# A planned instruction order that accounts for the SBUF port of GpSimd and VectorE, with first-layer weight sums moved into the attention part

## The chip, the cores and the metric

The kernel runs on one core of a Trainium2 chip. TensorE (PE) multiplies matrices, VectorE (DVE) and ScalarE (ACT) do elementwise work and read the matmul results in PSUM, GpSimd (POOL) does elementwise work on SBUF alone, and SyncE (SP) issues the DMAs. Each engine runs its own instructions in the order of the program and waits on semaphores for the others. The metric is device time in microseconds from the first to the last instruction; of several runs the median counts.

## The reference

An attention with decay is followed by a token mix and a dense layer pair; all weights of the second part (`U`, `V`, `w_ch1`, `w_ch2`) come as 64-bit floats, all else as 32-bit floats.

```python
batch, n_heads, seq, head_dim = (8, 8, 576, 64)          # d_model 512, rank 32
def _attn_ref(q, k, v, f):
    scores = scale * np.matmul(q, k.transpose(0, 1, 3, 2))
    cum = np.cumsum(np.log(np.clip(f, 0.0001, 1.0)), axis=-1)
    scores = np.where(causal, -1000000000.0, scores + cum[:, :, :, None] - cum[:, :, None, :])
    attn = np.exp(scores - np.max(scores, axis=-1, keepdims=True))
    attn = attn / (np.sum(attn, axis=-1, keepdims=True) + 1e-09)
    return np.matmul(attn, v)
def _moe_ref(x, U, V, w_ch1, w_ch2):                      # x: (8, 576, 512)
    u = x + (x.transpose(0, 2, 1) @ U @ V).transpose(0, 2, 1)
    return u + np.maximum(u @ w_ch1, 0.0) @ w_ch2         # 512 -> 2048 -> 512
```

## The kernel before, in words

A matmul operand is held as a high part and a low part (names that end in h and l), and a product is three matmuls: high by high, low by high, high by low.

The first part works through 32 pairs of heads, four to a batch. A pair's scores go to PSUM (tiles `S`), VectorE adds the decay and mask `M` and finds the row limit `nm` (L543, and L578 for the last 64 rows), ScalarE takes the exponent (L549), PE turns the result (L616) into PSUM tiles `T`, and a copy brings it to `PT` (line L267, on ScalarE or VectorE). PE multiplies by the values, and the normalised result lands in `xn`. `split_x` splits it, `ranks` makes the rank sums `TS` (L724 on VectorE). When a batch has its four pairs, `mix` adds the token mix to `xn` (PE L733, VectorE L734) and turns the result (PE L749, and L760 for the last 64 rows) into `uh` (a copy) and `ul` (L742 on VectorE). `dense` then does the first 6 of the 16 hidden chunks for that batch: L795 into PSUM, `hh` by ScalarE, `hl` by VectorE (L799), L816 back, and `ost` (L833). This dense work of the batch before is what PE does between the attention matmuls of the next.

The other ten chunks of both weights are prepared meanwhile by `ahead(r, i)` (r is 1 for the first layer's weight): 64-bit words are loaded into `araw`, decoded and stored to DRAM as `wd`. A decode, `decode_ops`, is a chain: a scaling (L375 on VectorE), `signs` (L385, L386) and `rest` (L390, L391), both on VectorE alone, an addition (L401), a copy (L409 or L410) and a subtraction (L405); the last three and the scaling may go to one of two engines. After the attention the second part loads `wd`, and `weight_sums` makes four sums per pair of first-layer chunks, which a block scheme with seven products uses in the third part, up to the end.

None of this order is written out. `op` notes a piece of work with its keys, its priority and its engines with a duration for each. `run` keeps a clock for each engine and again and again takes, over all engines, the piece that could begin first, by these durations and a fixed lag per engine; `fn()` then writes its instructions. So the order on each engine is fixed when the program is built, and on the chip nothing but semaphores for data keeps two engines in step. While dense work has not begun, `run` fills planned waits of PE with dummy matmuls (`keep_awake`, L856).

Of the kernel before, what the change touches and what calls it, by code (L numbers as in the profile page):

```python
# [48 lines left out]
def tile_decay_attention_moe(ctx, tc, qk, v, f, U, V, w1, w2, out):  # L49
# [312 lines left out]
    def decode_ops(pr, n, get, kr, ka, kw, rows=slice(0, 128)):  # L362
# [45 lines left out]
        op([
            ("ACT", 0.06 + 0.5 * k, lambda: nc.scalar.copy(views()[5], views()[3])),  # L409
            ("DVE", 0.06 + 0.27 * k, lambda: nc.vector.tensor_copy(views()[5], views()[3])),  # L410
        ], pr, ka, kw)
        op(both(low), pr, ka, kw)
# [549 lines left out]
    staged = [0]  # L962

    def weight_sums(i, pr):
        free = xn[(B - 2) % NX]
        homes = ((free[:, 2], X(B - 2, 2)), (free[:, 3], X(B - 2, 3)), (xn[(B - 3) % NX][:, NM], X(B - 3, NM)))
        a0, a1 = (xn[(B - 3) % NX][:, (2 * k + 1) % NM] for k in (2 * i, 2 * i + 1))
        k0, k1 = (X(B - 3, (2 * k + 1) % NM) for k in (2 * i, 2 * i + 1))
        for k, a, ka in ((2 * i, a0, k0), (2 * i + 1, a1, k1)):
            h, l = (w[k].bitcast(F32).rearrange("p c f -> p (c f)") for w in (b1h, b1l))  # L970
            whole = lambda e, a=a, h=h, l=l: e.tensor_tensor(a, h, l, op=ALU.add)
            op([("POOL", 1.23, lambda whole=whole: whole(nc.gpsimd)), ("DVE", 0.6, lambda whole=whole: whole(nc.vector))], pr, [("b1", k, x) for x in range(2)], ka)
        lo, hi = slice(0, 256), slice(256, 512)
        t = [free[:, x // 2, 256 * (x % 2) : 256 * (x % 2) + 256] for x in range(4)]
        ks = [X(B - 2, x // 2, x % 2) for x in range(4)]
        ops = (
            (0, t[0], a1[:, lo], a1[:, hi], ALU.add, k1), (1, t[1], t[0], a0[:, lo], ALU.subtract, k0 + ks[0]),
# [616 lines left out]
```

## Time and profile before

| what | value |
| --- | --- |
| median of 3 runs | 1205.87 us (1203.4 to 1208.3) |
| the profiled execution | 1211.09 us, of which its instructions span 1209.3 us |
| busy over the span | PE 96%, VectorE 63%, ScalarE 58%, GpSimd 32% |
| mean granted TensorE clock | 0.986 |

The first part fills the span up to about 690 us, the seven-product part most of what follows 790 us. A busy PE is not PE at its peak, since matmuls overlap and their ends are modelled; the waits of PE and the stretches in which its clock was halved tell more than the busy share.

### The profile page before, as it was taken

To read this page: it belongs to the slowest core of one execution; us is meant where nothing else is said; L and a number is where in the kernel's file an instruction comes from. 1 tells how busy PE (TensorE), PEld (TensorE's weight loads), DVE (VectorE), ACT (ScalarE), POOL (GpSimd) and SP (SyncE) were. 2 spreads that over 40 slices of the span, in tenths; PEclk is the share of its full clock that TensorE was granted. 3 is DMA by queue.
4 is the path that set the end of the run, shared out by engine and by line. 5 is a ranking of instruction groups with operands and counts; after the bars stand their busy time and mean duration, and the time that the engine had idled before them with its cause. 6 is when DMAs were issued, how large, how long until landed. Compare 5 with 4: busy or idle time off the path is not lost.

```text
span 1209.3 us, 23833 instructions
## 1 busy us (share of the span) xinstructions
PE 1163.5 (96%) x8370; PEld 1005.7 (83%) x8370; DVE 767.4 (63%) x1856; ACT 699.3 (58%) x1891; POOL 385.1 (32%) x512
## 2 busy tenths in 40 slices
PE   9889999999999999989999899999999999999998
PEld 5557778877868878778887798888999999999997
DVE  7888676575573664764654322248768778687765
ACT  8776666666765666655756321146555655555553
POOL 5676644555643554543633353100000000000000
PEclk9989999999999999989999999999999999999999
DMA  6654546656555355454451576647765564654643
GB/s 206 169 172 160 170 135 180 164 162 189 175 144 199 112 192 180 136 194 134 131 162 34 168 247 217 222 156 246 253 207 181 168 236 153 231 197 153 201 114 105
DMA packets 133448, 210.32 MB, mean 174 GB/s; under 512 B 16656, under 2 KB 58896, under 8 KB 131280
## 3 DMA queue, kind: packets, MB, share of 16 engines
q1 hardware_dynamic: 133056, 208.53, 55.1%
q8 instruction: 66, 1.08, 0.4%
q14 instruction: 54, 0.44, 0.1%
q10 hardware_dynamic: 272, 0.26, 0.1%
HBM read 153.03 MB, written 55.72 MB: 173 GB/s over the span
## 4 chain that ended last, share of the span: by engine, by line
PE 75%; DVE 11%; issue 4%; ACT 4%; DMA 3%; POOL 1%; SPq 1%; POOLq 0%; DVEq 0%; ACTq 0%
PE pf L1234 16%; PE F L795 9%; PE po L1326 8%; PE F L816 7%; PE T L653 6%; PE px L1326 4%; PE S L525 4%; PE T L616 3%; PE F L1052 2%; PE O L1074 2%; PE pf L1326 2%; DVE S L543 2%; ACT P L549 2%; PE po L1341 2%; PE T L635 1%
## 5 line engine op out<-in xcount | busy, mean ns | idle before, releaser
L549 ACT ACTIVATE P<-S,nm 128x512 f32<-128x512 f32 (+3 forms) x256 | 133.0, 530 | 58.0 <-DVE nm L543 57.6
L543 DVE CUSTOM_DVE_ANT_0 S<-S,M 128x512 f32<-128x512 f32 (+3 forms) x256 | 119.7, 516 | 53.3 <-PE S L525 46.3
L1385 POOL TENSOR_TENSOR xn<-xn,xn 128x512 f32<-128x512 f32 x1 | 1.3, 1267 | 411.7 <-DMA out_dram<-xn 411.7
L501 POOL TENSOR_SCALAR_AFFINE_SELECT M<-decay 128x1024 f32<-128x1024 f32 (+1 forms) x124 | 96.0, 788 | 106.6 <-DVE nm L543 88.9
L267 ACT COPY PT<-T 128x512 f32<-128x512 f32 (+4 forms) x282 | 113.6, 449 | 24.6 <-PE T L616 13.7
L795 PE MATMUL F<-uh,w1h 128*128 128x256 f32 (+1 forms) x352 | 113.7, 323 | 7.1 <-DVE hl L799 5.3
L795 PE MATMUL F<-uh,w1l 128*128 128x256 f32 (+1 forms) x352 | 106.0, 301 | 0.0
L795 PE MATMUL F<-ul,w1h 128*128 128x256 f32 (+1 forms) x352 | 106.0, 301 | 0.0
L616 PE MATMUL T<-ident,P 128*128 128x128 f32 x612 | 88.8, 279 | 8.0 <-ACT PT L267 2.4
L1457 ACT COPY ost<-pf 128x512 f32<-128x512 f32 x70 | 41.1, 587 | 87.3 <-PE pf L1234 87.3
L653 PE MATMUL T<-PT,vr 128*64 128x320 f32 (+3 forms) x628 | 91.1, 437 | 0.0
L616 PEld LDWEIGHTS T<-ident,P 128*128 128x128 f32 x612 | 71.3, 142 | 22.6 <-ACT PT L267 5.0
L1457 ACT COPY mc<-pf 128x512 f32<-128x512 f32 x69 | 40.5, 587 | 81.6 <-PE pf L1234 81.6
L484 POOL TENSOR_TENSOR qkl<-raw,qkh 128x576 fp32r<-128x576 f32 (+1 forms) x52 | 79.8, 1538 | 18.8 <-ACT qkh L483 13.1
L799 DVE SCALAR_TENSOR_TENSOR hl<-F,hh 128x256 fp32r<-128x256 f32 (+1 forms) x88 | 39.6, 451 | 69.2 <-ACT hh L804 68.6
L653 PEld LDWEIGHTS T<-PT,vr 128*64 128x64 f32 x628 | 41.2, 139 | 46.3 <-issue 35.8
L795 PEld LDWEIGHTS F<-uh,w1h 128*128 128x128 f32 x352 | 69.6, 198 | 11.5 <-DVE hl L799 6.2
L816 PE MATMUL F<-w2h,hh 128*128 128x512 f32 x180 | 77.1, 428 | 0.1
L704 POOL TENSOR_TENSOR xl<-xn,xh 128x512 fp32r<-128x512 f32 x32 | 42.2, 1320 | 91.4 <-ACT xh L701 48.9
L816 PE MATMUL F<-w2l,hh 128*128 128x512 f32 x180 | 71.1, 395 | 0.0
L816 PE MATMUL F<-w2h,hl 128*128 128x512 f32 x180 | 70.5, 392 | 0.0
L795 PEld LDWEIGHTS F<-uh,w1l 128*128 128x128 f32 x352 | 69.5, 198 | 0.0
(330 smaller groups left out, 3618.0 us busy)
## 6 DMA issues: line engine op xcount, KB each, us to landing
un<-ud SPq DMA_DIRECT2D x16, 1024.0 KB, 6.8
decay<-cumd SPq DMA_DIRECT2D x30, 512.0 KB, 5.9
d<-ud SPq DMA_DIRECT2D x48, 256.0 KB, 4.0
araw<-in_w_dram SPq DMA_DIRECT2D x20, 512.0 KB, 4.3
wd<-araw SPq DMA_DIRECT2D x20, 512.0 KB, 3.3
twd<-xn SPq DMA_DIRECT2D x40, 256.0 KB, 2.8
raw<-in_qk_dram SPq DMA_DIRECT2D x32, 288.0 KB, 4.1
Th<-twd SPq DMA_DIRECT2D x35, 256.0 KB, 3.3
```

The lines of the kernel that those rows point to most:

```text
L267: return [("ACT", 0.133 + 0.00068 * n, lambda: nc.scalar.copy(dst(), src())), ("DVE", 0.064 + 0.00104 * n, lambda: nc.vector.tensor_copy(d ...
L484: op([("POOL", 0.1 + 0.00225 * n, lambda c=c: nc.gpsimd.tensor_tensor(l[:, c], raw[:, c], h.bitcast(F32)[:, c], op=ALU.subtract))], p - 0. ...
L501: nc.gpsimd.affine_select(Ms[i], decay[:, :, 0:w], [[0, 2], [-1, w]], ALU.is_ge, MASKED, base=P * i, channel_multiplier=1)
L543: nc.vector.tensor_tensor_reduce(ps, ps, Ms[i][:, j], scale=-SCALE, scalar=3.0e38, op0=ALU.add, op1=ALU.min, accum_out=nm[:, col : col + 1],)
L549: nc.scalar.activation(PP[i][j], bank[j][:, off : off + w], AF.Exp, bias=nm[:, col : col + 1], scale=-1.0, accum_out=sm[:, col : col + 1])
L616: nc.tensor.transpose(bank[:, P * x : P * x + P], PP[i][j][:, P * c : P * c + P], ident)
L653: nc.tensor.matmul(ps, vr[:, c, j], PT[:, j, c, lo:hi], start=c == 0, stop=lo == 0)
L795: nc.tensor.matmul(bank[:, :nt], wt[:, fc, c], ut[:, c, sl], start=m == 0, stop=m == 3 * NDC - 1)
L816: nc.tensor.matmul(bank[:, :], ht[:, fc, P * y : P * y + P], wt[:, fc], start=fc == 0 and m == 0, stop=fc == NA - 1 and m == 2,)
L1234: nc.tensor.matmul(ps, a[x][:, c], b[y][:, c], start=start and m == 0, stop=m == 5, skip_group_check=True)
L1326: nc.tensor.matmul(ps[:, HT * x : HT * x + HT], f[a][:, P * x : P * x + P], w[b], start=k.i == 0 and m == 0 and x == 0 and not (k.n == NG ...
L1457: nc.scalar.copy(mc, FA)
```

## The change

It has four parts. (1) In the planner, GpSimd does not begin before the stretch in which VectorE holds the shared SBUF port has passed (`hold["DVE"]`), and a VectorE piece that carries a fourth number, the time for which it holds the port, does not begin before GpSimd is done (`hold["POOL"]`). (2) Durations on VectorE are raised, every result counts as ready 0.1 us later for its readers (`CUSH`), a decode step's another 0.4 us (`EASE`; 1.2 us behind the scaling, which reads a DMA's landing), and a change of PE's mode costs more priority (`TURN`). (3) The rule `LAZY` goes, by which VectorE took a piece that another engine may do only where that engine was 0.6 us behind. (4) `weight_sums` goes; `sums_ahead` makes the same sums from the decoded chunks while they are still in SBUF, behind every second first-layer chunk, and the order of the chunks is changed so that two first-layer ones stand together.

```diff
-TURN = 0.08
+TURN = 0.15
...
 SHY = 0.6
-LAZY = {"ACT": 0.6, "POOL": 0.6}
+EASE = 0.4
+CUSH = {"PE": 0.1, "DVE": 0.1, "ACT": 0.1, "POOL": 0.1, "SP": 0.1}
+BEHIND = 1.0
+AT, SPAN = 7, 22
...
+                    for eng, dur, fn, *port in o.alts:
                         if eng != e:
                             continue
-                        if e == "DVE" and len(o.alts) > 1:
-                            other = "ACT" if o.alts[0][0] == "ACT" or o.alts[1][0] == "ACT" else "POOL"
-                            if clock[other] < max(now, o.ready) + LAZY[other]:
-                                continue
                         est = max(now, o.ready)
+                        if e == "POOL":
+                            est = max(est, hold["DVE"])
+                        if port:
+                            est = max(est, hold["POOL"])
...
             clock[e] = end
+            if e == "POOL":
+                hold["POOL"] = end
+            if port:
+                hold["DVE"] = est + port[0]
...
-                    x.ready = max(x.ready, done)
+                    x.ready = max(x.ready, done + x.ease + CUSH[x.alts[0][0]])
...
-        op([("DVE", 0.1 + 0.9 * k, signs)], pr, (), ka + kr)
-        op([("DVE", 0.1 + 0.9 * k, rest)], pr, ka, kr)
+        op([("DVE", 0.14 + k, signs, 0.43 * k)], pr, (), ka + kr, ease=ease)
+        op([("DVE", 0.14 + k, rest, 0.43 * k)], pr, ka, kr, ease=ease)
 
         def both(fn):
-            return [("POOL", 0.1 + 1.13 * k, lambda: fn(nc.gpsimd)), ("DVE", 0.06 + 0.54 * k, lambda: fn(nc.vector))]
+            return [("POOL", 0.14 + 1.13 * k, lambda: fn(nc.gpsimd)), ("DVE", 0.08 + 0.6 * k, lambda: fn(nc.vector), 0.69 * k)]
 
...
-        ka = [("araw",)]
+        ka = [("araw", x) for x in range(3)]
+        own, ko = ((late_a, ("warm",)), (late_b, ("late",)))[r and i % 2]
         load(pr - 0.5, 512e3, lambda: nc.sync.dma_start(araw, (w1_src if r else w2_src)(NA + i)), w=ka)
         h, l = (araw[:, DM * x : DM * x + DM].bitcast(F32R) for x in range(2))
-        decode_ops(pr, 512, lambda: (araw.rearrange("p (n t) -> p n t", t=2), late_a[:, :], h, l), ka, [("warm",)], ka)
+        decode_ops(pr, 512, lambda: (araw.rearrange("p (n t) -> p n t", t=2), own[:, :], h, l), ka, [ko], ka, ease=EASE)
         load(pr, 524e3, lambda: nc.sync.dma_start(wd[r, i].rearrange("x p d -> p x d"), araw.bitcast(F32).rearrange("p (x d) -> p x d", x=2)), r=ka, w=[("wd", r, i)])
+
+    def sums_ahead(m, pr):
+        lo, hi = slice(0, 256), slice(256, 512)
+        fl32 = lambda t, sl: t[:, sl].bitcast(F32)
+        t = [lambda: fl32(araw, lo), lambda: fl32(araw, hi), lambda: fl32(late_b, lo), lambda: fl32(late_a, hi)]
+        b_hi, a_lo = lambda: fl32(late_b, hi), lambda: fl32(late_a, lo)
+        kt = [("araw", 0), ("araw", 1), ("late",), ("warm",)]
+
+        def both(n, fn):
+            return [("POOL", 0.14 + 1.13 * n, lambda: fn(nc.gpsimd)), ("DVE", 0.08 + 0.6 * n, lambda: fn(nc.vector), 0.69 * n)]
+
+        for n, x, y, o, kr in (
+            (0, t[2], b_hi, ALU.add, [("late",)]), (1, t[0], a_lo, ALU.subtract, [("araw", 0), ("warm",)]),
+            (2, a_lo, t[2], ALU.subtract, [("warm",)]), (3, t[3], t[1], ALU.subtract, [("araw", 1)]),
+        ):
+            op(both(0.5, lambda e, n=n, x=x, y=y, o=o: e.tensor_tensor(t[n](), x(), y(), op=o)), pr, kr, [kt[n]], ease=EASE)
+        homes = ((araw[:, 512:1024].bitcast(F32), ("araw", 2)), (spare_home, ("sum",)))
+        for x in range(4):
+            q, kh = homes[x % 2]
+            qr = q.bitcast(F32R)
+            op([("ACT", 0.36, lambda x=x, qr=qr: nc.scalar.copy(qr[:, lo], t[x]()))], pr, [kt[x]], [kh], ease=EASE)
+            low = lambda e, x=x, q=q, qr=qr: e.tensor_tensor(qr[:, hi], t[x](), q[:, lo], op=ALU.subtract)
+            op(both(0.5, low), pr, [kt[x]], [kh], ease=EASE)
+            load(pr, 262e3, lambda x=x, q=q: nc.sync.dma_start(twd[0, m, x], q), r=[kh], w=[("twd", m, x)])
 
...
-            TURNS.setdefault(7 + k * 22 // (2 * NB), []).append((1 - k % 2, k // 2))
+            TURNS.setdefault(AT + k * SPAN // (2 * NB), []).append((1 - k % 4 // 2, k // 4 * 2 + k % 2))
...
-                    ahead(r, i, p + 1.0)
+                    ahead(r, i, p + BEHIND)
+                    if r and i % 2:
+                        sums_ahead(i // 2, p + BEHIND)
...
-    def weight_sums(i, pr):
-        free = xn[(B - 2) % NX]
...
-            if i % 2:
-                weight_sums(i // 2, 41.0 + i)
```

Other durations are changed alike. Counted over the whole program, VectorE has 216 more instructions and ScalarE 167 fewer, GpSimd 59 fewer: 148 copies and 5 casts of L267 move from ScalarE to VectorE, as do 12 casts and 2 scalings of decodes, and 29 additions and subtractions of decodes and `split_x` move from GpSimd to VectorE. PE's instructions are the same but for 18 more dummy matmuls and as many weight loads, and the order on PE is nearly the same. The lines of the changed kernel stand some 10 lower (L742 is L752 there), and tile numbers behind a name differ.

At the end of the attention, VectorE's order before was this (the `mix` of the last batch; `xn_98` is that batch, `b1h` and `b1l` are the second part's weights, which DMAs bring):

```order
L833 TENSOR_TENSOR ost_134<-F_144,xn_97 128x512 [waits DMAHW7_49,PE_49]
L734 TENSOR_TENSOR xn_98<-S_138,xn_98 128x512 [waits PE_49,Pool_49]
L734 TENSOR_TENSOR xn_98<-S_139,xn_98 128x512 [waits PE_49]
L734 TENSOR_TENSOR xn_98<-S_140,xn_98 128x512 [waits PE_49]
L734 TENSOR_TENSOR xn_98<-S_141,xn_98 128x512 [waits PE_49]
L971 TENSOR_TENSOR xn_99<-b1h_7306,b1l_7316 128x512 [waits DMAHW4_49,DMAHW3_49,Pool_49]
L742 TENSOR_TENSOR ul<-F_145,uh 128x4x128 [waits DMAHW0_49,Activation_49]
L742 TENSOR_TENSOR ul<-T_142,uh 128x4x128 [waits Activation_49]
L734 TENSOR_TENSOR xn_98<-F_144,xn_98 64x512 [waits DVE_49,PE_49]
L742 TENSOR_TENSOR ul<-S_138,uh 128x4x128 [waits Activation_49]
```

and in the changed kernel it is this:

```order
L734 TENSOR_TENSOR TS<-T_145,TS 32x256 [waits Activation_49]
L744 TENSOR_TENSOR xn_98<-S_142,xn_98 128x512 [waits PE_49,Pool_49]
L843 TENSOR_TENSOR ost_136<-F_147,xn_97 128x512 [waits DMAHW0_49,PE_49]
L744 TENSOR_TENSOR xn_98<-S_143,xn_98 128x512 [waits PE_49]
L744 TENSOR_TENSOR xn_98<-S_141,xn_98 128x512 [waits PE_49]
L752 TENSOR_TENSOR ul<-S_140,uh 128x4x128 [waits DMAHW6_49,Activation_49]
L744 TENSOR_TENSOR xn_98<-T_144,xn_98 128x512 [waits PE_49]
L744 TENSOR_TENSOR xn_98<-T_145,xn_98 64x512 [waits DVE_49,PE_49]
L272 CAST uh<-F_147 128x4x128 [waits PE_49]
L752 TENSOR_TENSOR ul<-S_142,uh 128x4x128 [waits Activation_49]
L752 TENSOR_TENSOR ul<-F_147,uh 128x4x128 [waits DVE_49]
L752 TENSOR_TENSOR ul<-S_143,uh 128x4x128 [waits Activation_49]
```

The sum of two loaded weights (L971) that stood among the `mix` steps is gone, and one of the `uh` copies is VectorE's now.

In the `mix` of a middle batch (the sixth), VectorE's order before was this (`araw` and `w2a` are a decode's):

```order
L385 TENSOR_SCALAR araw<-araw 128x512 [waits DMAHW6_49,DMAHW0_49,Pool_49]
L386 SCALAR_TENSOR_TENSOR w2a<-w2a,araw 128x512 [waits DVE_49]
L742 TENSOR_TENSOR ul<-F_145,uh 128x4x128 [waits Activation_49]
L742 TENSOR_TENSOR ul<-F_144,uh 128x4x128 [waits Activation_49]
L578 ISA S_141,nm_126<-S_141,Mt,nm_126 128x288 [waits Pool_49]
L578 ISA nm_126 128x1
L390 TENSOR_SCALAR araw<-w2a 128x512 [waits DVE_49]
L391 SCALAR_TENSOR_TENSOR araw<-araw 128x512 [waits DVE_49]
L742 TENSOR_TENSOR ul<-F_145,uh 128x4x128 [waits Activation_49]
L742 TENSOR_TENSOR ul<-F_144,uh 128x4x128 [waits Activation_49]
```

and now this:

```order
L272 COPY PT<-T_145 128x4x128 [waits PE_49]
L272 CAST uh<-F_146 128x4x128 [waits PE_49]
L752 TENSOR_TENSOR ul<-F_147,uh 128x4x128 [waits Activation_49]
L752 TENSOR_TENSOR ul<-F_146,uh 128x4x128 [waits DVE_49]
L553 ISA S_140,nm_128<-S_140,M_110 128x384 [waits PE_49]
L553 ISA nm_128 128x1
L553 ISA S_141,nm_128<-S_141,M_110 128x384 [waits PE_49]
L553 ISA nm_128 128x1
L272 COPY PT<-T_144 128x128 [waits Activation_49]
L752 TENSOR_TENSOR ul<-F_147,uh 128x4x128 [waits Activation_49]
L752 TENSOR_TENSOR ul<-F_146,uh 128x4x128 [waits Activation_49]
```

The four decode instructions are gone from between the `ul` steps, to a place behind them; copies to `PT` and `uh` stand there instead.

Ahead of the rank sums of the first batch, `TS`, VectorE had this before:

```order
L604 RECIPROCAL rv_130<-sm_127 128x10 [waits Activation_49,Pool_49]
L375 TENSOR_SCALAR w2a<-xn_99 128x512 [waits DMAHW4_49]
L385 TENSOR_SCALAR xn_99<-xn_99 128x512 [waits DVE_49]
L386 SCALAR_TENSOR_TENSOR w2a<-w2a,xn_99 128x512 [waits DVE_49]
L390 TENSOR_SCALAR xn_99<-w2a 128x512 [waits DVE_49]
L391 SCALAR_TENSOR_TENSOR xn_99<-xn_99 128x512 [waits DVE_49]
L724 TENSOR_TENSOR TS<-T_142,TS 32x256 [waits PE_49,Activation_49]
```

and now this:

```order
L272 COPY PT<-T_144 128x4x128 [waits PE_49]
L272 COPY PT<-T_145 128x2x128 [waits PE_49]
L400 TENSOR_SCALAR xn_99<-xn_99 128x512 [waits DVE_49]
L401 SCALAR_TENSOR_TENSOR xn_99<-xn_99 128x512 [waits DVE_49]
L272 COPY PT<-T_145 128x8x64 [waits PE_49,Activation_49]
L395 TENSOR_SCALAR xn_99<-xn_99 128x512 [waits DMAHW4_49,Activation_49]
L396 SCALAR_TENSOR_TENSOR w2a<-w2a,xn_99 128x512 [waits DVE_49]
L734 TENSOR_TENSOR TS<-T_144,TS 32x256 [waits Activation_49]
```

Five decode instructions in a row ahead of `TS` have become two, with copies ahead of those.

## Rows read from the trace of the kernel before

**Rows 1.** Busy time by stretch: engines busy in us (instructions), clock, DMA share, GB/s.
```profile
0.00:130.00 130.00, 115.65 (x749) 78.22 (x751) 103.70 (x261) 95.45 (x277) 85.04 (x116) 0.96 0.58 174
130.00:660.00 530.00, 511.16 (x3663) 417.67 (x3660) 320.21 (x856) 339.97 (x984) 254.53 (x338) 0.99 0.52 157
660.00:860.00 200.00, 193.73 (x1090) 167.58 (x1091) 87.05 (x197) 69.29 (x174) 44.22 (x57) 0.98 0.62 206
```

**Rows 2.** Waits of PE: waiting group, releaser, us in total, times, longest.
```profile
PE F L795 <- DVE hl L799: 5.3, 4, 1.9
PE F L760 <- DVE ul L742: 3.7, 2, 3.0
PE S L760 <- DVE xn L734: 3.7, 1, 3.7
PE F L733 <- DVE TS L724: 3.3, 1, 3.3
PE F L749 <- DVE ul L742: 2.8, 2, 1.7
PE T L616 <- ACT PT L267: 2.4, 6, 0.9
...
PE T L616 <- DVE TS L724: 2.2, 2, 1.3
...
PE T L616 <- DVE PT L267: 1.5, 3, 0.8
```

**Rows 3.** Stretches of half clock: columns as in Rows 1.
```profile
80.03:86.84 6.81, 5.37 (x18) 2.39 (x20) 5.20 (x17) 3.35 (x10) 6.15 (x8) 0.50 0.55 162
...
359.93:366.73 6.80, 6.55 (x32) 6.43 (x33) 3.85 (x6) 3.54 (x10) 3.77 (x5) 0.50 1.06 315
537.42:544.22 6.80, 6.60 (x32) 6.48 (x33) 2.31 (x6) 2.67 (x7) 1.89 (x4) 0.50 1.01 378
694.43:701.24 6.81, 6.63 (x26) 5.93 (x27) 2.50 (x6) 1.47 (x4) 1.78 (x3) 0.50 0.80 285
```

**Rows 4.** PE in order of time, 684 to 700 us: start, us, what, idle.
```profile
694.61 0.69 PE L760 MATMUL S<-ident,xn 64*128 64x64 f32 x4 [3.68 <-DVE xn L734]
```

**Rows 5.** VectorE in order of time, 684 to 696 us.
```profile
685.74 2.48 DVE L734 TENSOR_TENSOR xn<-S,xn 128x512 f32<-128x512 f32 x4
692.08 0.69 DVE L971 TENSOR_TENSOR xn<-b1h,b1l 128x512 f32<-128x512 f32 x1 [3.86 <-DMA b1l<-wd]
```

**Rows 6.** VectorE in order of time, 528 to 538 us.
```profile
533.98 1.04 DVE L390 TENSOR_SCALAR araw<-w2a 128x512 int32<-128x512 int32 x1
535.06 1.91 DVE L391 SCALAR_TENSOR_TENSOR araw<-araw 128x512 f32<-128x512 uint32 x1
```

**Rows 7.** GpSimd in order of time, 529 to 538 us.
```profile
533.32 3.09 POOL L484 TENSOR_TENSOR qkl<-raw,qkh 128x576 fp32r<-128x576 f32 x2 [1.44 <-ACT qkh L483]
```

**Rows 8.** PE in order of time, 528 to 538 us.
```profile
537.62 0.69 PE L760 MATMUL F<-ident,xn 64*128 64x64 f32 x4 [2.95 <-DVE ul L742]
```

**Rows 9.** VectorE in order of time, 296 to 303 us.
```profile
301.47 0.43 DVE L390 TENSOR_SCALAR araw<-w2a 128x512 int32<-128x512 int32 x1
301.94 0.69 DVE L391 SCALAR_TENSOR_TENSOR araw<-araw 128x512 f32<-128x512 uint32 x1
```

**Rows 10.** VectorE by line and shape, 0 to 760 us: busy, mean ns | idle.
```profile
L391 DVE SCALAR_TENSOR_TENSOR araw<-araw 128x512 f32<-128x512 uint32 x20 | 17.8, 889 | 0.7
...
L390 DVE TENSOR_SCALAR araw<-w2a 128x512 int32<-128x512 int32 x20 | 15.3, 767 | 0.2
...
L267 DVE COPY PT<-T 128x512 f32<-128x512 f32 x8 | 5.5, 688 | 1.1 <-PE T L616 1.0
```

**Rows 11.** Groups of the whole span, GpSimd: busy, mean ns | idle.
```profile
L981 POOL TENSOR_TENSOR xn<-xn,xn 128x256 f32<-128x256 f32 x10 | 7.4, 736 | 0.3
```

**Rows 12.** PE in order of time, 74 to 84 us.
```profile
77.52 0.61 PE L856 MATMUL F<-ident 128*128 128x256 bf16 x4
81.47 1.22 PE L733 MATMUL F<-TS,VV 128*128 128x512 f32 x2 [3.34 <-DVE TS L724]
```

More of the change, by code (lines that the diff above doesn't have):

```diff
@@ L186, in tile_decay_attention_moe @@
     araw = sb.tile([P, 1024], I32, tag="araw", name="araw")
+    late_b = sb.tile([P, 512], I32, tag="w2b", name="w2b")
+    spare_home = sb.tile([P, DM], F32, tag="sums", name="sums")
     NMX = [sb.tile([P, 10], F32, tag=f"nm{x}", name=f"nm{x}") for x in range(2)]
@@ L222, in tile_decay_attention_moe, with op @@
     class Op:
-        __slots__ = ("alts", "pr", "opens", "uses", "mode", "needs", "gives", "ready", "lands", "n", "end", "group")
-    def op(alts, pr, r=(), w=(), opens=(), uses=(), mode=None, lands=None, behind=()):
+        __slots__ = ("alts", "pr", "opens", "uses", "mode", "needs", "gives", "ready", "lands", "n", "end", "group", "ease")
+    def op(alts, pr, r=(), w=(), opens=(), uses=(), mode=None, lands=None, behind=(), ease=0.0):
         o = Op()
@@ L242, in op @@
         need.discard(o)
-        o.needs = 0
+        o.needs, o.ease = 0, ease
         for k in behind:
@@ L274, in tile_decay_attention_moe @@
     free = {x: 0.0 for x in range(8)}
+    hold = {"DVE": 0.0, "POOL": 0.0}
     def run(*groups):
@@ L310, in run @@
                             pr += TURN
-                        cand.append((est, pr, o.n, o, dur, fn, homes))
+                        cand.append((est, pr, o.n, o, dur, fn, homes, port))
                 if not cand:
@@ L318, in run @@
             assert best is not None, [(o.pr, o.needs) for o in todo if o.end is None][:20]
-            est, e, (_, _, _, o, dur, fn, homes) = best
+            est, e, (_, _, _, o, dur, fn, homes, port) = best
             if e == "PE":
@@ L360, in X, with decode_ops @@
         return [("x", b % NX, i, h) for h in ((0, 1, 2, 3) if hp is None else (hp,))]
-    def decode_ops(pr, n, get, kr, ka, kw, rows=slice(0, 128)):
+    def decode_ops(pr, n, get, kr, ka, kw, rows=slice(0, 128), ease=0.0):
         k = n / 512
@@ L405, in low @@
             e.tensor_tensor(l[rows], af[rows], h.bitcast(F32)[rows], op=ALU.subtract)
-        op(both(add), pr, kr, ka)
+        op(both(add), pr, kr, ka, ease=ease)
         op([
[L409 to L412, printed above, removed]
+            ("ACT", 0.1 + 0.5 * k, lambda: nc.scalar.copy(views()[5], views()[3])),
+            ("DVE", 0.08 + 0.37 * k, lambda: nc.vector.tensor_copy(views()[5], views()[3]), 0.43 * k),
+        ], pr, ka, kw, ease=ease)
+        op(both(low), pr, ka, kw, ease=ease)
     def weights(u):
@@ L707, in rows @@
             e.tensor_tensor(xh[64:128, NM, hs], x[0:64, NM, fs], xh.bitcast(F32)[0:64, NM, hs], op=ALU.subtract)
-        op([("POOL", 1.23, lambda: low(nc.gpsimd)), ("DVE", 0.6, lambda: low(nc.vector))], pr, kx + [("xh", hp % 2)], [("xl", hp % 2)])
-        op([("POOL", 0.46, lambda: rows(nc.gpsimd)), ("DVE", 0.29, lambda: rows(nc.vector))], pr, kx, [("xh", hp % 2)])
+        op([("POOL", 1.23, lambda: low(nc.gpsimd)), ("DVE", 0.68, lambda: low(nc.vector), 0.69)], pr, kx + [("xh", hp % 2)], [("xl", hp % 2)])
+        op([("POOL", 0.46, lambda: rows(nc.gpsimd)), ("DVE", 0.29, lambda: rows(nc.vector), 0.29)], pr, kx, [("xh", hp % 2)])
     def ranks(b, half, pr):
@@ L960, in block2 @@
         return [w[2 * i + r - 1][:, 256 * (c - 1) : 256 * c] for w in (b2h, b2l)]
-    staged = [0]
-    def weight_sums(i, pr):
-        free = xn[(B - 2) % NX]
[L966 to L977, printed above, removed]
-            (2, t[2], a0[:, lo], a1[:, lo], ALU.subtract, k0 + k1), (3, t[3], a0[:, hi], t[1], ALU.subtract, k0 + ks[1]),
-        )
-        for n, dst, x, y, o, kr in ops:
-            both = lambda e, dst=dst, x=x, y=y, o=o: e.tensor_tensor(dst, x, y, op=o)
-            op([("DVE", 0.34, lambda both=both: both(nc.vector)), ("POOL", 0.66, lambda both=both: both(nc.gpsimd))], pr, kr, ks[n] + (X(B - 2, n // 2) if n in (0, 2) else []))
-        for x in range(4):
-            h, kh = homes[staged[0] % 3]
-            staged[0] += 1
-            q = h.bitcast(F32R)
-            op([("ACT", 0.31, lambda q=q, x=x: nc.scalar.copy(q[:, lo], t[x]))], pr, ks[x], kh)
-            low = lambda e, q=q, x=x: e.tensor_tensor(q[:, hi], t[x], q[:, lo].bitcast(F32), op=ALU.subtract)
-            op([("DVE", 0.34, lambda low=low: low(nc.vector)), ("POOL", 0.66, lambda low=low: low(nc.gpsimd))], pr, ks[x], kh)
-            load(pr, 262e3, lambda h=h, x=x: nc.sync.dma_start(twd[0, i, x], h), r=kh, w=[("twd", i, x)])
     with tc.manual_schedule(engines=None):
```

7 lines of the change are left out of this document (3 added, 4 removed).

## The prediction

> **What bounds the kernel now.** I looked first at the busy time by stretch [rows 1]. PE is busy in nearly all of the 530 us from 130 to 660 (511.2), VectorE in 320.2 and GpSimd in 254.5. So no engine but PE is full there, and since the change leaves PE its instructions, only PE's waits, its clock and its slow begin can move the time. From 860 on nothing is touched.
>
> Next come PE's waits [rows 2]. Nearly all of them end on VectorE, and on few kinds of instruction: `hl` 5.3 us, `ul` 3.7 + 2.8 = 6.5, `TS` 3.3 + 2.2 = 5.5, one on `xn` 3.7, and 1.5 on VectorE's copies to `PT`. Copies on ScalarE cost 2.4. Then the clock: there are four stretches of 6.8 us in which the granted clock is 0.50 [rows 3], the lower of its two levels, 1.2 GHz. At half speed 3.4 us of PE's time are lost in each. Each begins within 2 us of the end of a longer wait of PE, three of which have rows below: on `TS` up to 81.47 [rows 12], on `ul` up to 537.62 [rows 8], and on `xn` up to 694.61 [rows 4]; the fourth, at 359.93, follows two waits on `ul`. These waits therefore cost double.
>
> What is late in them? At 694.61 PE has stood 3.68 us for `xn` [rows 4]. On VectorE, four steps of `mix` were done at 688.2; then a weight sum, L971, stood at the head of the queue for 3.86 us, for a DMA that brings `b1l` [rows 5]. Behind it waited `ul` and the last `xn` step, and PE behind these. This is a wait in a queue, not work.
>
> The waits inside the attention are another kind. Around 534, L390 took 1.04 us and L391 behind it 1.91 [rows 6], while GpSimd ran two subtractions from 533.32 to 536.41 [rows 7]; the `ul` that stood behind them let PE go on at 537.62, 2.95 us late [rows 8]. With GpSimd out of the way the same two took 0.43 and 0.69 [rows 9]. Over the 20 late chunks L390 means 767 ns and L391 889 [rows 10]. So a decode step is lengthened where GpSimd runs beside it, and PE waits where one stands ahead of what it needs.
>
> **The change, part by part.** *The weight sum at the end.* No L971 is left on VectorE, and in the changed order no instruction there reads a freshly loaded weight. The 3.7 us of wait go, and with the wait the drop of the clock, 3.4: **-7.1**. The sums' other work after 690, on GpSimd and ScalarE, was waited for by nobody in [rows 2], and is worth nothing by itself. What is late next is `ul` there; in the changed order six matmuls of the dense part stand ahead of it at each step. The bounds are -3.7, if the clock falls anyway, and -7.1.
>
> *Where the decode steps stand.* I counted VectorE's whole order: for how many instructions that PE waits for do two or more decode, split or sum instructions stand directly ahead. Before it is `hl` 13, `ul` 7, `TS` 5, `xn` of `mix` 2, `ost` 5; after, 10, 1, 6, 6 and 5. The price of a place is what [rows 2, 3] give to that kind. `ul`: 6.5 and two clock stretches of 3.4, 13.3 over 7 places, of which 6 go: -11.4. `hl`: 5.3 over 13, 3 go: -1.2. `TS`: 5.5 and 3.4, 8.9 over 5, one more: +1.8. `xn`: four more; no wait behind a decode there shows before, so I take the mean of the other three kinds without the clock, (5.3 + 6.5 + 5.5) / 25 = 0.7 each: +2.8. Together **-8.0**; the bounds are 0, if waits just move elsewhere, and -12.6, if the added places cost nothing.
>
> *The turns at the port.* Of waits and clock behind decode steps, 17.3 + 10.2 - 8.0 = 19.5 are left. How much shorter do the steps get? Against the free durations, L390 is lengthened by 0.34 and L391 by 0.20 on average. The plan's hold for `signs` and `rest` is 0.43 us, which is the first instruction alone, so it sees 0.34 of 0.54, 63%. It works only where both engines keep the plan's time, since no semaphore holds either back. I take a quarter of the 19.5: **-5**, between 0 and 63%, -12.3.
>
> The Trainium skill, SBUF — State Buffer, section Who interferes with whom, says the shared port pair is an exclusive lock, taken for a whole instruction by whichever begins first, and that a VectorE instruction with two SBUF inputs contends with a GpSimd one that reads SBUF. The trace agrees [rows 6, 7]: L391 has two such inputs and ended 0.6 us behind GpSimd. By that rule L391 gains nothing from the hold, and the 29 additions and subtractions that come over from GpSimd contend too; the turns would be worth 0 instead of -5. This is the second rival below.
>
> *More work on VectorE.* 148 copies come over from ScalarE; at 688 ns for the largest [rows 10] and less for the others, about 0.45 on average, that is 66 us. The 43 pieces of decodes and splits that change engine and 20 more sums add some 30. In the stretch from 130 to 660, with about 90 of them, VectorE goes from 60% to 77%. The price: PE waited 1.5 us for VectorE's `PT` copies, of which there were 27, 0.056 each, so 148 make +8.2; for ScalarE's 282 it waited 2.4, so 148 fewer make -1.3. That leaves -1.3 to +6.9; I take **+3**, the middle. For the other 30 us: 18.8 us of waits on VectorE in the attention over 424 us of its busy time [rows 1, 2] is 0.044 per us: **+1**.
>
> *The sums within the attention.* Some 19 of them on GpSimd at 0.74 us [rows 11] are 14 us beside 254.5 busy of 530; 20 copies and 20 stores lie beside ScalarE and queues that are half idle. Nothing, as long as the stores are not late; if they are, see the fourth rival. *The 18 dummies*: four of them took 0.61 us, right in front of the wait for `TS` of 3.34 [rows 12]; they fill time in which PE stands, so 0, at most +2.7.
>
> The sum is -7.1 - 8.0 - 5 + 3 + 1 = -16.1. Against the profiled execution's 1211.09 that gives 1195.0, of whose time 1.8 lie outside the span; that execution is 5.2 above the median, 1205.87, from which the same sum gives **1190**.
>
> **The rivals.** *All waits on VectorE go*, with their clock stretches: 22.5 + 13.6 = 36 off, 1170. For it speaks that every one has a cause that the plan now knows; against it, that the chip keeps no plan to 0.1 us.
>
> *The turns do not hold and the waits only change place.* Then the end's 7.1 are the gain and the 4 of the added work the loss: 1203, no change. For it speaks the rule above; against it, that `ul`, which cost most, has no decode ahead of it now.
>
> *VectorE becomes the bound: slower.* If pieces came to it at random, waits would grow like load over idle share, from 0.60 / 0.40 = 1.5 to 0.77 / 0.23 = 3.3, by 2.2 times: 18.8 becomes 41, +22.6, less 7.1 gives 1221. It decides from a load of 67%, at which that growth eats the 7.1. Against it: the order is planned, and puts the copies where VectorE would idle.
>
> *A DMA at the head of VectorE's queue.* Each `araw` now serves the decode, the sums and the stores in turn, and the last decode begins during the last pair. If one load is late, VectorE stands as it did for L971, at the same 7.1: 1197.
>
> **How the numbers follow.** This kernel's three runs differ by 0.4%, so some 0.5%, 6 us, is what can be told from no change: below 1199.8 is faster, above 1211.9 slower. Chances: forecast 0.52, all waits gone 0.06, no change 0.18, VectorE the bound 0.14, a late DMA 0.10. Of the forecast 0.50 is on the faster side, of the late DMA 0.07: faster 0.63, same 0.21, slower 0.16. The range leaves out half of the best case, the slow one and a little beside: 1174 to 1208. The likeliest case alone spans 1180 to 1199.
>
> **What would show it.** Right: no idle PE near 690 and no half clock behind it; waits on `ul` under 1.5 us in all, one or two stretches of half clock; L390 under 600 ns on average; VectorE near 77% from 130 to 660. Wrong: L391 still near 890 ns, waits on `hl`, `xn` or `PT` copies over 15 us, or a wait of VectorE on `araw` of some microseconds, with PE idle behind it.

## The result, and the profile after

The changed kernel takes **1174.09 us** (median of 4 runs, 1173.78 to 1174.59) beside 1206.04 for the kernel before: a ratio of 0.9736, interval 0.9716 to 0.9756, or 32 us less. Its profiled execution took 1174.59 us with a span of 1172.6, 36.7 shorter than the 1209.3 of before; that is more than 32, since the profiled execution of before lies 5 us above its median. One execution of a run below, e2, took 1851.98 us at a mean granted clock of 0.557; e2's ratio leaves it out, its median of six does not (1198.53 without it).

The busy time by stretch of the changed kernel, with the columns of [rows 1], and in the first row the only stretch of half clock left between 30 and 760 us:

```profile
482.49:485.89 3.40, 3.40 (x13) 2.12 (x12) 1.53 (x5) 2.91 (x10) 1.36 (x3) 0.50 0.52 181
...
0.00:130.00 130.00, 124.02 (x860) 87.58 (x860) 117.81 (x307) 98.35 (x287) 86.38 (x115) 1.00 0.65 191
130.00:660.00 530.00, 520.71 (x3765) 427.31 (x3765) 391.58 (x1058) 295.96 (x867) 236.71 (x338) 1.00 0.55 166
660.00:860.00 200.00, 197.87 (x1192) 176.16 (x1191) 101.51 (x222) 70.18 (x164) 0.00 (x0) 1.00 0.65 214
```

VectorE went from 320.21 to 391.58 us in the middle stretch, 74% of it, and PE still gained 9.6 us of busy time there: VectorE did not become the bound. In place of the stretches of [rows 3] there is one of 3.40 us.

The waits of PE in the changed kernel from 30 to 700 us (waiting group, releaser, us in total, times, longest), which answer to [rows 2]:

```profile
PE F L759 <- DVE ul L752: 2.2, 3, 1.1
PE F L826 <- DVE hl L809: 1.8, 2, 1.5
PE T L645 <- DVE TS L734: 1.7, 2, 1.4
PE F L743 <- DVE xn L744: 0.8, 1, 0.8
PE T L626 <- DVE PT L272: 0.7, 1, 0.7
```

All rows of this view added give 33.3 us in 37 waits before and 11.8 in 22 now, 21.5 less. The granted clock was 0.50 for 30.7 us before (the four stretches of [rows 3] and one of 3.4 us) and for 3.4 now, of which half is lost: 13.7 less. Together that is 35.2 of the 36.7 us. By releaser, the waits on VectorE fell from 26.1 to 10.0 us and those on ScalarE from 7.2 to 1.8. No kind of wait has taken the place of another.

At the end of the attention, PE and then VectorE in order of time, where [rows 4, 5] had 3.68 us without work:

```profile
660.78 0.60 PE L759 MATMUL S<-ident,xn 128*128 128x128 f32 x4
661.31 0.46 PE L770 MATMUL S<-ident,xn 64*128 64x64 f32 x4
661.70 0.50 PE L826 MATMUL F<-w2h,hh 128*128 128x512 f32 x1
```
```profile
659.75 1.27 DVE L744 TENSOR_TENSOR xn<-T,xn 128x512 f32<-128x512 f32 x2
660.98 0.69 DVE L272 CAST uh<-F 128x512 fp32r<-128x512 f32 x1
661.59 0.68 DVE L752 TENSOR_TENSOR ul<-S,uh 128x512 fp32r<-128x512 f32 x1
```

None of these rows ends in a bracket, so nobody waits, and no half clock follows.

VectorE by line and shape from 0 to 760 us (busy, mean ns, idle), answering to [rows 10]:

```profile
L272 DVE COPY PT<-T 128x512 f32<-128x512 f32 x51 | 34.5, 685 | 10.5 <-PE T L645 9.3 <-PE T L652 1.0 <-PE T L626 0.2
...
L401 DVE SCALAR_TENSOR_TENSOR araw<-araw 128x512 f32<-128x512 uint32 x20 | 16.1, 804 | 0.7
...
L400 DVE TENSOR_SCALAR araw<-w2a 128x512 int32<-128x512 int32 x15 | 6.4, 427 | 0.1
...
L400 DVE TENSOR_SCALAR araw<-w2b 128x512 int32<-128x512 int32 x5 | 2.1, 411 | 0.1
```

The instruction that was L390 fell from 767 ns to its free length of [rows 9], 0.43 us. The one behind it, L401, only fell from 889 to 804.

### The profile page after: what moved, and what is told of

Read it like the earlier page. It is cut to its first block, busy times and chain, and to the rows that moved or that the text cites. A ratio compares the mean times of both kernels' runs of the same rounds, so it can differ in the third digit from the quotient of the medians.

```text
span 1172.6 us, 23731 instructions
## 1 busy us (share of the span) xinstructions
PE 1149.2 (98%) x8388; PEld 997.5 (85%) x8388; DVE 841.1 (72%) x2072; ACT 638.1 (54%) x1724; POOL 324.4 (28%) x453
## 5 line engine op out<-in xcount | busy, mean ns | idle before, releaser
L805 PE MATMUL F<-uh,w1h 128*128 128x256 f32 (+1 forms) x344 | 106.7, 310 | 0.7 <-DVE ost L843 0.3
L805 PE MATMUL F<-uh,w1l 128*128 128x256 f32 (+1 forms) x344 | 101.1, 294 | 0.0
L272 DVE COPY PT<-T 128x512 f32<-128x512 f32 (+4 forms) x148 | 71.1, 500 | 37.4 <-PE T L626 17.6
L663 PE MATMUL T<-PT,vr 128*64 128x448 f32 (+2 forms) x624 | 88.7, 430 | 0.4 <-ACT PT L272 0.4
L826 PE MATMUL F<-w2h,hh 128*128 128x512 f32 x198 | 84.5, 427 | 1.8 <-DVE hl L809 1.8
L272 ACT COPY PT<-T 64x128 f32<-64x128 f32 (+4 forms) x157 | 64.0, 430 | 35.9 <-PE T L626 11.8
L826 PE MATMUL F<-w2l,hh 128*128 128x512 f32 x198 | 78.5, 396 | 0.0
L826 PE MATMUL F<-w2h,hl 128*128 128x512 f32 x198 | 77.7, 393 | 0.0
L1239 PE MATMUL pf<-d,b1h 128*128 128x256 f32 x320 | 69.5, 280 | 0.0
L814 ACT ACTIVATE hh<-F 128x256 fp32r<-128x256 f32 (+1 forms) x86 | 34.9, 412 | 56.6 <-PE F L805 56.4
```

The source lines that it names most:

```text
L272: return [("ACT", 0.133 + 0.00068 * n, lambda: nc.scalar.copy(dst(), src())), ("DVE", 0.064 + 0.00104 * n, lambda: nc.vector.tensor_copy(d ...
L663: nc.tensor.matmul(ps, vr[:, c, j], PT[:, j, c, lo:hi], start=c == 0, stop=lo == 0)
L805: nc.tensor.matmul(bank[:, :nt], wt[:, fc, c], ut[:, c, sl], start=m == 0, stop=m == 3 * NDC - 1)
L826: nc.tensor.matmul(bank[:, :], ht[:, fc, P * y : P * y + P], wt[:, fc], start=fc == 0 and m == 0, stop=fc == NA - 1 and m == 2,)
L1239: nc.tensor.matmul(ps, a[x][:, c], b[y][:, c], start=start and m == 0, stop=m == 5, skip_group_check=True)
```

## The experiments

Two words first: *turns* are the two rules with `hold`, and *room* is the time by which `CUSH` and `EASE` let a result count as ready later. The theory with which I went on: the gain is PE's waits on VectorE with their clock, 7 to 8 us of it the weight sum at the end, the rest the turns, through shorter decode steps that stand in better places. The rivals: the gain comes from the free choice of engine, which takes copies off ScalarE; or from the room behind results, for which the prediction had no term. All kernels at a glance: median and ratio to the kernel before that ran on the same chip, PE's waits from 30 to 700 us (all rows of the view added), and the time at half clock from 30 to 760 us. The last column is the span less the waits and half of the time at half clock.

| kernel | us | ratio, interval | waits | half clock | rest |
| --- | --- | --- | --- | --- | --- |
| before | 1206.04 | 1 | 33.3 | 30.7 | 1160.6 |
| changed | 1174.09 | 0.9736, 0.9716 to 0.9756 | 11.8 | 3.4 | 1159.1 |
| before, end sums not on VectorE (e5) | 1200.51 | 0.9942, 0.9923 to 0.9962 | 29.9 | 23.9 | 1160.4 |
| changed, sums late as before (e4) | 1177.26 | 0.9754, 0.9727 to 0.9780 | 13.4 | 10.2 | 1157.7 |
| changed, sums late, not on VectorE (e9) | 1170.75 | 0.9691, 0.9670 to 0.9712 | 9.6 | 0 | 1159.4 |
| changed, no turns (e2) | 1198.69 | 0.9938, 0.9916 to 0.9961 | 29.7 | 6.8 | 1164.0 |
| changed, no room (e3) | 1194.49 | 0.9902, 0.9873 to 0.9932 | 24.2 | 13.7 | 1162.2 |
| changed, neither (e11) | 1207.86 | 1.0000, 0.9988 to 1.0011 | 36.2 | 20.5 | 1161.2 |
| before, with room 0.1 (e8) | 1196.60 | 0.9912, 0.9893 to 0.9930 | 25.5 | 20.5 | 1160.1 |
| changed, with LAZY (e1) | 1179.53 | 0.9777, 0.9744 to 0.9809 | 16.9 | 0 | 1160.2 |
| before, without LAZY (e6) | 1213.82 | 1.0056, 1.0041 to 1.0071 | 37.0 | 17.1 | 1166.5 |
| changed, longer hold (e7) | 1176.55 | 0.9737, 0.9717 to 0.9756 | 12.8 | 3.4 | 1159.0 |
| changed, no turns, longer steps planned (e12) | 1186.08 | 0.9828, 0.9813 to 0.9843 | 17.3 | 10.2 | 1162.1 |
| changed, CUSH 0.11 (e10) | 1172.58 | 0.9711, 0.9686 to 0.9736 | 9.4 | 0 | 1160.3 |

The last column is the first finding. Over fourteen kernels, whose times differ by 43 us, it stays between 1157.7 and 1166.5. What moves the time most is PE's waits and the clock behind them; what they leave unexplained is up to 9 us, with e6 and e2 at the upper end. The runs were made on several chips, on which the median of the kernel before went from 1206.04 to 1208.34, so a difference between two rows' medians is uncertain by some 2 us; the ratios compare on one chip.

**The nudge (e10).** It tells how much a mere reshuffle of the order moves the time.

```diff
-CUSH = {"PE": 0.1, "DVE": 0.1, "ACT": 0.1, "POOL": 0.1, "SP": 0.1}
+CUSH = {"PE": 0.11, "DVE": 0.11, "ACT": 0.11, "POOL": 0.11, "SP": 0.11}
```

> The changed kernel with the room behind every result at 0.11 us in place of 0.10: no theory gives it a meaning, but the planned order changes in many places. It shows how far the time moves with the order alone: within 3 us of 1174 if single steps can be read from differences of 5 us and more.

It came out at 1172.58, 1.5 less, or 3.0 by the ratios. Differences of 2 or 3 us between two orders therefore carry no meaning by themselves.

**The weight sum at the end (e5, e4, e9).** In e5 the sums of whole weights in the kernel before may go to GpSimd alone:

```diff
-            op([("POOL", 1.23, lambda whole=whole: whole(nc.gpsimd)), ("DVE", 0.6, lambda whole=whole: whole(nc.vector))], pr, ...
+            op([("POOL", 1.23, lambda whole=whole: whole(nc.gpsimd))], pr, ...
```

> The kernel before with one edit: the sum of two loaded weights may run on GpSimd alone, so the one such sum leaves VectorE's queue; the planned order is else the same. By the first term of the forecast PE's wait of 3.7 us near 691 goes and the clock stays up behind it: 7.1 us less, 1199. If the clock falls anyway, 3.7 less, 1202.5; if another wait takes the place, 1206.

Measured: 1200.51 beside 1208.34, 7.8 less, and from 600 us on none of the waits of [rows 4, 5] is left. In e4 the changed kernel gets `weight_sums` of before back in place of `sums_ahead`, and in e9 the same with all of these sums on GpSimd:

```diff
-                    if r and i % 2:
-                        sums_ahead(i // 2, p + BEHIND)
...
+            if i % 2:
+                weight_sums(i // 2, 41.0 + i)
```

> The changed kernel with the weight sums made after the attention again (the old function), 25 of them on VectorE. By the forecast's first term a sum that waits for a loaded weight stands in VectorE's queue among the steps of the last batch: a wait of PE near 655 and half clock behind it, 7 us more, 1181. If that wait was an accident of one order, 1174.

> The changed kernel with the weight sums after the attention, as in the fourth experiment, but on GpSimd and ScalarE alone, so that none stands in VectorE's queue. If the wait of 4.5 us and the half clock behind it were VectorE's queue, 7.9 us less than the fourth: 1169, below the changed kernel. If the sums in the attention cost nothing, no gain over the changed kernel: 1174.

VectorE, PE and the stretch behind them in e4:

```profile
660.04 0.69 DVE L1006 TENSOR_TENSOR xn<-b1h,b1l 128x512 f32<-128x512 f32 x1 [4.52 <-DMA b1l<-wd]
```
```profile
662.58 0.69 PE L770 MATMUL S<-ident,xn 64*128 64x64 f32 x4 [4.48 <-DVE xn L744]
```
```profile
661.97:668.77 6.80, 6.19 (x24) 5.49 (x25) 3.28 (x6) 1.13 (x4) 1.09 (x2) 0.50 0.87 308
```

The wait of [rows 4, 5] is back, row by row: 4.48 us of PE behind a DMA at the head of VectorE's queue, and the half clock. That is 4.48 + 3.4 = 7.9 us in the trace, and 6.5 between the medians of e4 and e9 (7.6 by the ratios), which differ in this alone and have the same order up to the last steps of the attention. The changed kernel is 3.3 slower than e9 (5.4 by the ratios), a little more than a nudge gives. That would be why e4 lies between my two cases: the wait costs its 7 us or so, and sums that are no longer in the attention give part of it back. e9, at 1170.75, is the fastest of all these kernels.

**Turns and room, each alone and neither (e2, e3, e11, e8).** e2 leaves out the four lines of the turns, e3 sets the room to 0, e11 does both, and e8 gives 0.1 us of room to the kernel before, with nothing else of the change.

```diff
-                        if e == "POOL":
-                            est = max(est, hold["DVE"])
-                        if port:
-                            est = max(est, hold["POOL"])
```
```diff
-EASE = 0.4
-CUSH = {"PE": 0.1, "DVE": 0.1, "ACT": 0.1, "POOL": 0.1, "SP": 0.1}
+EASE = 0.0
+CUSH = {"PE": 0.0, "DVE": 0.0, "ACT": 0.0, "POOL": 0.0, "SP": 0.0}
```
```diff
-                    x.ready = max(x.ready, done)
+                    x.ready = max(x.ready, done + 0.1)
```

> The changed kernel without the two turn rules (GpSimd does not wait for VectorE's hold in the plan, nor VectorE for GpSimd). If the turns shorten decode steps, L400 and L401 on araw grow back to some 770 and 890 ns and PE waits more on ul and hl: 1182 to 1192. If two engines that nothing keeps in step do not hold the turns, lengths and time stay: 1171 to 1178.

> The changed kernel without the room behind results (CUSH and EASE at 0). If the room keeps an engine from standing at the head of its queue for a late result, PE's waits grow and the time rises to 1180 to 1190; if it is the turns and the places alone, 1171 to 1178.

> The changed kernel without the two rules of the turns and without the room behind results; sums in the attention, the new durations and the free choice of engine stay. If turns and room are worth what each cost when it alone was taken out (24.6 and 20.4 us over 1174.1), and each by itself, both together cost 45 and give about 1219. If they are one thing, a plan that the chip keeps only when it has both, the second one taken away costs little more: 1195 to 1203.

> The kernel before with 0.1 us of room behind every result, and nothing else of the change (weight sums after the attention as before, LAZY kept, no turns, no further room behind decode steps). If the room is a gain by itself, most of the 20.4 us that its removal cost: 1186 to 1192. If it works only together with the turns, within 6 us of the kernel before.

From the four medians: without both 1207.86; room alone brings 9.2, turns alone 13.4, both 33.8, which is 11.2 more than the sum (by the ratios 7.5, 11.8 and 31.8, which is 12.5 more). So neither of my two expectations for e11 held: they are not two separate gains of 24.6 and 20.4, nor one thing that needs both. e2 and e3 cost more than I had thought at most (1192 and 1190). Room alone on the kernel before brings 11 us (e8), about as much as in e2 and between the two cases that I had for it. And with neither, all the rest of the change together is worth nothing: 1.0000. That fits its parts as far as they were measured: 7.8 us gained at the end (e5) and 6.2 lost by the free choice of engine (e6).

Without the turns the collision of [rows 6 to 8] returns in the same batch. VectorE, GpSimd and PE in e2:

```profile
527.23 1.38 DVE L396 TENSOR_SCALAR araw<-w2a 128x512 int32<-128x512 int32 x1
528.64 1.91 DVE L397 SCALAR_TENSOR_TENSOR araw<-araw 128x512 f32<-128x512 uint32 x1
530.47 0.68 DVE L748 TENSOR_TENSOR ul<-F,uh 128x512 fp32r<-128x512 f32 x1
```
```profile
526.91 3.08 POOL L490 TENSOR_TENSOR qkl<-raw,qkh 128x576 fp32r<-128x576 f32 x2
```
```profile
531.20 0.50 PE L766 MATMUL F<-ident,xn 64*128 64x64 f32 x4 [2.40 <-DVE ul L748]
```

L397 and L396 are the L391 and L390 of before, and stand for 3.3 us beside two subtractions of GpSimd. The `ul` behind them comes late, PE waits 2.40 us, and its clock falls at 531.5.

The waits of PE in e11, the kernel with neither:

```profile
PE T L622 <- ACT PT L272: 6.7, 7, 3.0
PE T L622 <- DVE PT L272: 3.3, 5, 1.1
PE T L648 <- DVE TS L730: 3.0, 3, 1.3
PE F L801 <- DVE hl L805: 2.7, 3, 1.7
```

They are another mixture than in [rows 2], with 10 us on the `PT` copies, and about the same sum.

**What the turns do (e7, e12).** e7 lets the hold for `signs` and `rest` cover both instructions. e12 has no turns, but plans these two at about the length that they have in e2.

```diff
-        op([("DVE", 0.14 + k, signs, 0.43 * k)], pr, (), ka + kr, ease=ease)
-        op([("DVE", 0.14 + k, rest, 0.43 * k)], pr, ka, kr, ease=ease)
+        op([("DVE", 0.14 + k, signs, 1.12 * k)], pr, (), ka + kr, ease=ease)
+        op([("DVE", 0.14 + k, rest, 1.12 * k)], pr, ka, kr, ease=ease)
```
```diff
...
-        op([("DVE", 0.14 + k, signs, 0.43 * k)], pr, (), ka + kr, ease=ease)
-        op([("DVE", 0.14 + k, rest, 0.43 * k)], pr, ka, kr, ease=ease)
+        op([("DVE", 0.14 + 1.5 * k, signs, 0.43 * k)], pr, (), ka + kr, ease=ease)
+        op([("DVE", 0.14 + 1.5 * k, rest, 0.43 * k)], pr, ka, kr, ease=ease)
```

> The changed kernel with the hold of signs and rest at 1.12 us in place of 0.43, so that the plan keeps GpSimd away from the second instruction too, which has two SBUF inputs. If that one is lengthened because no hold covers it, L401 falls from 804 ns to about 700 and the time by 1 to 4 us, to 1170 to 1173. If GpSimd's later begin costs more than that, 1175 to 1182.

> The changed kernel without the turns, but with signs and rest planned at 1.64 us in place of 1.14, about what they last there (0.64 + 0.84 for rest, 0.54 + 0.91 for signs). If the turns pay because the plan then knows how long a decode step lasts, a plan that knows it in this other way recovers most of the 24.6: 1175 to 1185. If they pay because the steps are really shorter, it recovers little: 1192 to 1200.

In e7, VectorE by line and shape:

```profile
L401 DVE SCALAR_TENSOR_TENSOR araw<-araw 128x512 f32<-128x512 uint32 x20 | 14.6, 730 | 0.7
...
L400 DVE TENSOR_SCALAR araw<-w2a 128x512 int32<-128x512 int32 x15 | 6.3, 421 | 0.1
```

The second instruction is shorter, as the longer hold should make it: L401 is at 730 ns in place of 804. The time is 1176.55, 2.5 more, at the same ratio. In e12 12.6 of the 24.6 us come back without any turn, about half; 1186.08 lies 1 us above the first of my two cases and 6 below the second.

Does the time follow the length of the decode steps, as my theory has it? For the 32 decode steps of 512 columns I averaged the four instructions of `signs` and `rest` and added the four means, and counted how many of the 64 of `rest` (L390 and L391, whatever their number) overlapped one of GpSimd:

| kernel | four means, us | overlaps of 64 | waits of PE, us |
| --- | --- | --- | --- |
| before | 3.02 | 40 | 33.3 |
| before, with room (e8) | 3.10 | 39 | 25.5 |
| neither (e11) | 3.08 | 35 | 36.2 |
| room (e2) | 3.08 | 33 | 29.7 |
| turns (e3) | 3.12 | 46 | 24.2 |
| room, longer steps planned (e12) | 2.91 | 47 | 17.3 |
| both (changed) | 2.69 | 27 | 11.8 |
| both, longer hold (e7) | 2.48 | 13 | 12.8 |

Over the eight kernels it does not, and so shorter steps are not the whole of what the turns bring, as my theory had it. With turns and no room the chip does not keep the turns (46 overlaps, more than with no rule at all) and the steps are no shorter, and still 13.4 us are gained over e11. Room shortens nothing either, in e8 or e2, and gains 11 and 9.2. And e7, with the shortest steps, gains nothing. What is left for these gains is the order itself: what stands ahead of the things that PE waits for, and with how much time to spare. With room, steps and waits do fall together from e2 over e12 to the changed kernel, so there the two can't be told apart; in e12 the steps are 0.17 us shorter than in e2.

Is the order better by the planner's own clock, or does the chip keep it better? PE's last piece for the pairs of heads is the product `T<-xh,Us` of the rank sums. The planner in each kernel gives it a begin (`est` in `run`), and the trace has its begin on the chip. In the kernel before and in the changed one it begins here:

```profile
682.49 0.28 PE L719 MATMUL T<-xh,Us 128*64 128x256 f32 x1
```
```profile
652.92 0.28 PE L729 MATMUL T<-xh,Us 128*64 128x256 f32 x1
```

| kernel | planned, us | on the chip, us | late, us |
| --- | --- | --- | --- |
| before | 631.3 | 682.5 | 51.2 |
| before, with room (e8) | 635.2 | 674.7 | 39.4 |
| neither (e11) | 634.6 | 688.1 | 53.5 |
| room (e2) | 637.3 | 677.2 | 39.9 |
| turns (e3) | 639.9 | 673.1 | 33.2 |
| room, longer steps planned (e12) | 647.3 | 665.0 | 17.6 |
| both (changed) | 641.5 | 652.9 | 11.4 |
| both, longer hold (e7) | 643.4 | 654.7 | 11.3 |

By its own clock the plan of the changed kernel is 10 us longer than that of before (raised durations, turns and room all lengthen it), and the chip reaches this piece 30 us sooner. So turns and room do not make a shorter plan but one that the chip keeps more nearly.

**The free choice of engine (e1, e6).** e1 puts the rule LAZY back into the changed kernel, e6 takes it out of the kernel before.

```diff
+                        if e == "DVE" and len(o.alts) > 1:
+                            other = "ACT" if o.alts[0][0] == "ACT" or o.alts[1][0] == "ACT" else "POOL"
+                            if clock[other] < max(now, o.ready) + LAZY[other]:
+                                continue
```

> The changed kernel with the rule LAZY put back: VectorE has 79 copies in place of 180, ScalarE the others. If copies on VectorE are a load, as the forecast priced them (+3 us), the time falls by some 3 us, to about 1171. If sharing the copies is where the gain that was not forecast comes from, the time rises by 6 us or more, to 1180 to 1190, with waits of PE on ScalarE's copies.

> The kernel before without the rule LAZY alone, so that VectorE takes copies freely, with no turns and no room. The rule cost 5.4 us when put back into the changed kernel. If the free choice is a gain by itself, about 1200. If more work on VectorE helps only a plan that is kept, no change or slower, 1205 to 1215.

In the changed kernel the free choice is worth 5.4 us; in the kernel before it costs 6.2. In e1 the waits on ScalarE's copies to `PT`, which I had named for this case, did not grow: 1.1 us beside 1.0 in the changed kernel, while those on `ul` went from 2.2 to 4.8. So why the time rose there is not shown. The waits of PE in e6 from 30 to 700 us:

```profile
PE T L612 <- DVE PT L267: 8.4, 7, 1.7
PE F L756 <- DVE ul L738: 6.7, 5, 3.1
PE T L745 <- DVE xn L730: 4.4, 1, 4.4
```

The copies that come to VectorE are waited for, 8.4 us or 6.9 more than in [rows 2]; the prediction priced this at +8.2. In the changed kernel the same group is 0.7. But the waits on ScalarE's copies and on `hl` fell, so that all waits grew by 3.7 only (37.0 beside 33.3), and there is 13.6 us less of half clock. These rows therefore don't account for the 6.2 us, which stand on the medians alone; the last column of e6 is the highest of all. So the same edit has another sign in the changed kernel than in the kernel before, and the runs do not show by which step.

## Why the prediction came out as it did

The time fell into the range with 0.1 us to spare, and almost twice as far from before as the forecast of 16.1 us. That it lies inside is luck: the room, whose removal costs 20.4 us, was in no term, the copies had the wrong sign, and the lower end of the range came from half of a rival with a chance of 0.06. By its steps:

- **The weight sum at the end, -7.1.** Right: -7.8 in e5, -6.5 between e4 and e9, 7.9 in the rows of e4. The second half, that the clock goes with the wait, is right too.
- **Where the decode steps stand, -8.0.** The rule behind it failed. I priced a place by the wait that its kind had before. The same count, two or more decode, split or sum instructions ahead of something that PE waits for, gives 25 places for e11, 28 for the changed kernel, 33 for e7 and e9 and 39 for e12, whose waits are 36.2, 11.8, 12.8, 9.6 and 17.3 us; for the kernel before it gives 32, with 33.3 us. So a place has no price of its own. `ul` came out near its term, 6.5 us and two clock stretches became 2.2 and none; but `TS`, with a place more, fell from 5.5 to 2.3, and `xn` of `mix`, with four more, costs 1.3 in place of my 2.8.
- **The turns, -5 (0 to -12.3).** Too small, and by a wrong mechanism. What I expected of the steps came: L390 under 600 ns, L391 still long. But taking the turns out costs 24.6 us with the room there, and 13.4 without. e7 shortens the steps further for nothing, and e3 gains its 13.4 with steps no shorter than those of e11. So at least that part of the value of the turns lies in the order, not in shorter steps. How the 11.2 that turns and room bring only together split between shorter steps and order stays open.
- **The room behind results: no term.** This is the main omission. I listed `CUSH` and `EASE` as part of the change and gave them no price. Their removal costs 20.4 us, and 0.1 us of room alone brings the kernel before 11.
- **More copies on VectorE, +3, and other work, +1.** Wrong in sign: -5.4 (e1). I took the price of a copy from the kernel before, and in that kernel the sign holds (e6, +6.2), though its waits do not account for the size.
- **Sums within the attention, 0.** 3.3 us by the medians and 5.4 by the ratios (e9), a little more than what the nudge moves. The stores were not late, and VectorE has no wait on `araw` of a microsecond.

Of the rivals, the one that all waits on VectorE go with their clock (1170) was the nearest, and its chance of 0.06 was far too small. Of its 36 us some 26 went: the waits that it counted fell from 22.5 to 8.3 us, and the loss by the clock from 13.6 to 1.7. The other 9 of the 35.2 come from what this rival did not count, above all the waits on ScalarE, 5.4 us. The rival that the turns don't hold fell with e2. It rested on a rule of the Trainium skill, SBUF — State Buffer, section Who interferes with whom, that a VectorE instruction with two SBUF inputs contends with a GpSimd one that reads SBUF. The rows of e2 agree with the rule: GpSimd's subtractions ended at 529.99 and L397 at 530.55. But it speaks of one instruction's length, and the time hung on the order. VectorE as the bound (from a load of 67%) fell at 74%.

Four of my five signs for "right" came: no idle PE near 690 and no half clock behind it, one stretch of half clock, L390 under 600, VectorE near 77% (74). The fifth, waits on `ul` under 1.5 us, missed with 2.2.

That with room and turns the chip keeps nearer to the planned times is shown by the last piece of the attention, 51.2 us late before and 11.4 now. Why it does, and how much of it is room that takes up small delays, is argued and not shown.

## What to carry to other kernels

Before pricing edits to a planned order, add up the waits of the engine that bounds and the clock behind them: span less these was constant within 9 us over fourteen kernels, so their sum, 48.7 us in the profiled execution here, is about the whole prize, and a forecast for a better plan should reach to most of it. Small room behind every result (9 to 20 us), and planned lengths nearer to those on the chip (12.6 us, e12), were worth more than shorter instructions beyond that (nothing, e7), and room and turns more together than apart. A plan's own length says little: the better kernel had the longer plan. An edit that moves work to a fuller engine can change its sign from one kernel to another (5.4 us gained, 6.2 lost), so price it in the kernel that it will stand in; and keep an instruction that waits for a DMA out of the queue that the bounding engine waits for (6.5 to 7.9 us for one).

## What the hardware showed unexpectedly

- The length of a wait alone did not tell whether the clock falls. In e1 a wait of 1.9 us on `TS` was followed by none below full clock between 30 and 760 us, while in the changed kernel one of 1.48 us on `hl` was followed by 3.40 us at 0.50, the lower level, 1.2 GHz:

```profile
PE T L668 <- DVE TS L739: 1.9, 1, 1.9
```
```profile
481.89 0.50 PE L826 MATMUL F<-w2h,hh 128*128 128x512 f32 x1 [1.48 <-DVE hl L809]
```

- VectorE's copies from PSUM did not lengthen beside GpSimd: 688 ns on average over 8 before [rows 10], 685 over 51 now. Of these 51, the 41 that overlapped an instruction of GpSimd took 684 ns on average and the other ten 690, while the decode steps beside GpSimd went from 0.43 to 1.38 us and from 0.69 to 1.91 (e2).
